# Turning B and C on VectorE instead of TensorE in a fused Mamba-2 scan and ELU feed-forward kernel

## The chip, the cores and the metric

The kernel runs on one core of a Trainium2 chip. The core has a matrix engine (TensorE, PE in the profile), three engines for elementwise work (VectorE or DVE, ScalarE or ACT, GpSimd or POOL), a queue engine (SyncE or SP) that issues most transfers here, and 16 DMA engines. The metric is the time of one execution on the device in microseconds (us); smaller is better. A figure for a kernel is the median of several executions.

## The reference: what is computed

There are two stages. The first is a state-space scan over 4 batches, 8 heads and 768 tokens, with 32 values (x) and 16 state numbers (B and C) per head and token. Written in chunks it is

```
cum   = cumsum(log a)                        # inside a chunk, per head
M     = (C @ B.T) * exp(cum_i - cum_j)       # j <= i only
y     = M @ x  +  exp(cum_i) * (C @ state)
state = exp(cum_last) * state + sum_j exp(cum_last - cum_j) * B_j x_j
```

The second stage takes the 8 heads of a token side by side as a row of 256 numbers, and computes `elu(row @ w_in) @ w_out` with `w_in` 256x2048 and `w_out` 2048x256. The weights arrive as 64-bit floats and are made into 32-bit ones on the chip; everything else is 32-bit. The output is 3072 rows of 256.

## The kernel before

**Blocks.** The work is cut into 12 blocks of 256 tokens of one batch, numbered n = 0 to 11. Blocks 2k and 2k + 1 are a pair: the same third of two batches. Inside a block the scan works on chunks of 64 tokens; u (0 or 1) says which half of 128 tokens, v which chunk in it. For each block the scan goes through these steps, each a function of its own:

- `load_bc` (L106) loads B and C into the tile `bc`, tokens on the partitions, in four transfers of 64 KB. A run in memory is 16 floats, 64 bytes. The issues are at L112.
- `scaled` (L359) multiplies B by the decay to the chunk's end, on GpSimd. It needs tokens on the partitions.
- `turn` (L368) makes the other layout, head and state number on the partitions and tokens along the row. TensorE transposes four 128x128 squares into two PSUM tiles (L374); ScalarE copies B's to `bt` (L378); VectorE makes `ctm` (L381), C's rows in two versions, each with every second head masked to zero. C itself stays in PSUM.
- `turn_exp` (L385) multiplies that C by the decay `ec` into `cts` on VectorE (L389), which frees the PSUM tile.
- `scores` (L450) multiplies `bt` and `ctm` on TensorE, `weigh` (L465) applies the decays on VectorE, `sums` and `states` (L480, L496) carry the state on, `across` and `inside` (L522, L542) make the rows of y.

**The feed-forward part** is where most of TensorE's time goes. For blocks 0 to 3 it is done directly, by `l1` (L577, first product), `elu` (L598, two steps on ScalarE and one on VectorE that writes `g`, L605) and `l2` (L700). For blocks 4 to 11 the pairs are done with a scheme of seven part products per pair instead of eight: `front`, `mid` and `back` (L660 to L692) for the first product, with sums between them on VectorE (L673, L674, L682, L689, L690), and `second` (L736) for the second product, whose results are summed up at L750. `mid` ends with the VectorE sum L682, which reads a half of a PSUM bank; `back` then accumulates into that half.

**Order.** Nothing is planned automatically: the order of the calls in the code is the order of each engine's queue. There are three parts. A start (up to L951) brings in blocks 0 to 2 and converts weights; in it a loop over s (L914) runs `l1` for blocks 0 and 1. A loop over n = 2, 3 (L1011) does `l2` of the blocks two back with `l1` of its own. The pair loop, n = 4, 6, 8, 10 (L1051), has 16 steps k. In an even step stand `front`, its sums, an `elu` and four steps of `second`; in an odd step `mid`, two steps of `second`, `back`, one step, an `elu` and the start of another. After each step `scan_ahead` (L967) puts in a piece of the scan of the coming pair: in the pair loop loads at k = 0 and 1, `turn` and `turn_exp` at k = 5 (first block of the pair) and k = 7 (second block).

The turn of blocks 6, 8 and 10 is thus at k = 5 and of blocks 7, 9 and 11 at k = 7 of the pair loop at n = 4, 6 and 8. Block 2 is turned at s = 5 of the start, block 3 at i = 1 of n = 2, blocks 4 and 5 at i = 5 and 7 of n = 2.

The first products share seven PSUM tiles (tag "a"), which `turn` also takes two of.

Of the kernel before, what the change touches and what calls it, by code (L numbers as in the profile page):

```python
# [10 lines left out]
F32 = mybir.dt.float32  # L11
U32 = mybir.dt.uint32
BF16 = mybir.dt.bfloat16
ALU = mybir.AluOpType
ACT = mybir.ActivationFunctionType

P = 128
Q = 64
BLK = 2 * P
# [9 lines left out]
def kernel(  # L29
# [27 lines left out]
    nc = tc.nc  # L57
    NB, NH, S, D = x.shape
    N = B.shape[-1]
# [4 lines left out]
    DM, DF = moe_w_in.shape  # L64
# [6 lines left out]
    raw = ctx.enter_context(tc.tile_pool(name="raw", bufs=3))  # L71
    att = ctx.enter_context(tc.tile_pool(name="att", bufs=2))
    ffn = ctx.enter_context(tc.tile_pool(name="ffn", bufs=2))
# [5 lines left out]
    def psum(shape, name):  # L79
        return p_a.tile(shape, F32, tag="a", name=name)  # L80
# [6 lines left out]
    for k in range(4):  # L87
        (nc.scalar if k % 2 else nc.sync).dma_start(
            out=la0[BH * k:BH * (k + 1)],
            in_=a.rearrange("b h (c s) -> (b h) c s", s=P)[:, 0:2, :])  # L90
# [5 lines left out]
    st = {}  # L96

    def place(n):

        return 2 * (n // (2 * NG)) + n % 2, n // 2 % NG  # L100
# [5 lines left out]
    def load_bc(n, c_queue=nc.sync):  # L106
        b, g = place(n)
        st.setdefault(n, {})["bc"] = raw.tile([P, 2, 2, NH, N], F32, tag="bc", name="bc", bufs=2)
        for u in range(2):
            sl = slice((2 * g + u) * P, (2 * g + u + 1) * P)  # L110
            for k, src in enumerate((B, C)):
                (nc.sync, c_queue)[k].dma_start(  # L112
                    out=st[n]["bc"][:, k, u], in_=src[b, :, sl, :].rearrange("h s n -> s h n"))
# [118 lines left out]
    for v in range(2):  # L232
        nc.gpsimd.affine_select(
            out=low16[Q * v:Q * v + Q], in_=low16[Q * v:Q * v + Q], pattern=[[1, Q]],
# [5 lines left out]
        out=hmask, in_=hmask, pattern=[[-N, NH]], compare_op=ALU.is_ge, fill=0.0,  # L240
        base=0, channel_multiplier=1)
    nc.gpsimd.affine_select(
        out=hmask, in_=hmask, pattern=[[N, NH]], compare_op=ALU.is_ge, fill=0.0,
# [3 lines left out]
    hmask2 = const.tile([P, 2], F32, name="hmask2")  # L247
# [4 lines left out]
        out=minus, in0=ident, scalar1=-1.0, scalar2=None, op0=ALU.mult)  # L252
# [106 lines left out]
    def scaled(n, eng):  # L359

        s = st[n]
        s["sc"] = sc = att.tile([P, 2, NH, N], F32, tag="sc", name="sc", bufs=3)
        factor = eb0[:, :, NH * n:NH * (n + 1)] if n < 2 else eb[:, :, rows_of(n)]
        eng.tensor_tensor(
            out=sc, in0=s["bc"][:, 0],
            in1=factor.unsqueeze(3).to_broadcast([P, 2, NH, N]), op=ALU.mult)

    def turn(n):  # L368

        s = st[n]  # L370
        tb, tc_ = psum([P, 2, P], "ps_tb"), psum([P, 2, P], "ps_tc")
        for k, ps in enumerate((tb, tc_)):
            for u in range(2):
                nc.tensor.transpose(  # L374
                    out=ps[:, u], in_=s["bc"][:, k, u].rearrange("p h n -> p (h n)"),
                    identity=ident)
        s["bt"] = att.tile([P, 2, P], F32, tag="bt", name="bt", bufs=3)
        nc.scalar.copy(out=s["bt"], in_=tb)  # L378
        s["ct"] = tc_
        s["ctm"] = att.tile([P, 2, 2, P], F32, tag="ctm", name="ctm")  # L380
        nc.vector.tensor_tensor(  # L381
            out=s["ctm"], in0=tc_.unsqueeze(2).to_broadcast([P, 2, 2, P]),
            in1=hmask2.unsqueeze(1).unsqueeze(3).to_broadcast([P, 2, 2, P]), op=ALU.mult)

    def turn_exp(n):  # L385

        s = st[n]
        s["cts"] = att.tile([P, 2, P], F32, tag="cts", name="cts", bufs=3)
        nc.vector.tensor_tensor(out=s["cts"], in0=s.pop("ct"), in1=s["ec"], op=ALU.mult)  # L389

# [307 lines left out]
    def l2(n, j, half=None):  # L700


        if j == 0 and half != 1:
            o_of[n] = p_o.tile([P, 2, DM], F32, tag="o", name="ps_o")
        for m in (2 * j, 2 * j + 1) if half is None else (2 * j + half,):
            for ts in range(2):
                nc.tensor.matmul(  # L707
                    out=o_of[n][:, ts], lhsT=g_of[n, j][:, m % 2, ts * P:(ts + 1) * P],
                    rhs=w_out[:, m], start=(m == 0 and ts == 0), stop=(m == MC - 1),
                    skip_group_check=True)  # L710
        if j == MC // 2 - 1 and half != 0:
            ob = ffn.tile([P, 2, DM], F32, tag="ob", name="ob")
            nc.scalar.copy(out=ob, in_=o_of.pop(n))
            r0 = row_of(n)
            nc.sync.dma_start(
                out=out[r0:r0 + BLK, :].rearrange("(t p) e -> p t e", p=P), in_=ob)
# [197 lines left out]
    for s, (n, i) in enumerate((  # L914
            (1, 0), (1, 1), (1, 2), (0, 4), (1, 3), (0, 5), (1, 4), (0, 6), (1, 5), (0, 7),
            (1, 6), (1, 7))):
        l1(n, i)
        if s < 8:
            decay_of(2, s)
        if s == 7:  # L920
            scores(2)
            weigh(2, 0)
            weigh(2, 1)
        if s % 2 == 1 and todo < 10:
            w_take(todo, nc.vector)
            w_give(todo)
            w_load(todo + 6)
            todo += 1
        if s == 4:
            scaled(2, nc.gpsimd)  # L930
        if s == 5:
            turn(2)
            first_exp(2)
            turn_exp(2)
        if s == 8:
            spread_cum(3)
            load_x(3)
            spread_exp(3)
            weigh(2, 2)
            weigh(2, 3)  # L940

            st[0] = kept
            sums(2, 0, pool=p_o, tag="o", parts=(None, last))
            states(0, last)
            st.pop(0)
            states(2)
        if s == 10:
            spread_cum(4)
            inside(across(2), 2)
        if len(lag) > 1:  # L950
            elu()  # L951
# [15 lines left out]
    def scan_ahead(n, i):  # L967


        m = n + 2 + n % 2  # L970
        if 4 < m < NP and n % 2 == 1 and i in (4, 5):
            spread_cum(m + i - 4)
        m = n + 2 - n % 2
        if 4 <= m < NP and n % 2 == 0:
            if i < 2:
                load_bc(m + i)
                spread_exp(m + i)
            if i == 2:
                if m == 4:
                    spread_cum(5)  # L980
                load_x(m)
                load_x(m + 1)
            for k in (i,) if m == 4 else (i, i + 1) if i % 2 == 0 else ():
                if k >= 2:
                    decay(m + k // 6, (k - 2) % 4)
            if i in (5, 7):
                turn(m + i // 7)
                turn_exp(m + i // 7)
        if 4 <= m < NP and n % 2 == 1:
            if i == 0:  # L990
                scaled(m, nc.gpsimd)
                scaled(m + 1, nc.gpsimd)
            for k in (i,) if m == 4 else (i, i + 1) if i % 2 == 0 else ():
                if k < 2:
                    decay(m + 1, k + 2)
            if i == 2 and m == 4:
                scores(m, m + 1)
                sums(m, m + 1)
                for q in range(4):
                    weigh(m, q)  # L1000
                    weigh(m + 1, q)
                states(m)
                states(m + 1)
# [7 lines left out]
    for n in (2, 3):  # L1011
        for i in range(8):
            l2(n - 2, i)
            if todo < len(pieces):
                w_take(todo, nc.vector)
            end_of_two(n, 2 * i)
            l1(n, i)
            if todo < len(pieces):
                w_give(todo)
                w_load(todo + 6)  # L1020
                todo += 1
            while lag:
                elu()
            if n == 2:
                if i < 2:
                    decay(3, 2 * i)
                    decay(3, 2 * i + 1)
                if i == 1:
                    scaled(3, nc.gpsimd)
                    turn(3)  # L1030
                    turn_exp(3)
                if i == 2:
                    scores(3)
                    for q in range(4):
                        weigh(3, q)
                if i == 4:
                    sums(3)
                    states(3)
                if i == 6:
                    inside(across(3), 3)  # L1040
            else:
                if i == 0:
                    s_in[:], s_out[:] = weight_sums(), weight_sums()
                elif i < 7:
                    more_sums(i - 1)
            scan_ahead(n, i)
            end_of_two(n, 2 * i + 1)
# [3 lines left out]
    for n in range(4, NP, 2):  # L1051
        m = n + 2 if n + 2 < NP else None
# [13 lines left out]
        for k in range(16):  # L1066
            i = k // 2
# [54 lines left out]
    n = NP - 2  # L1122
# [41 lines left out]
```

## Time and profile before

The median of three executions is 364.41 us (364.31 to 366.16). The profiled execution spans 362.9 us.

| Operation | Engine, line | Number | Mean of one, ns |
|---|---|---|---|
| part product 128x128, 256 columns | PE L655 | 448 | 379 to 385 |
| second product, 128 columns | PE L759 | 1120 | 275 |
| transpose 128x128 | PE L374 | 48 | 273 to 275 |
| bt, copy out of PSUM, 128x256 | ACT L378 | 12 | 358 |
| scaled B, 128x256 | POOL L364 | 12 | 655 |
| M, 128x256 | DVE L468 | 48 | 413 |
| g, 128x512 | DVE L605 | 96 | 681 |

How to read it: the page gives busy times by engine, then the chain of work that ended last, then groups of instructions. The mean of one is from its start to its end; neighbouring instructions of one engine overlap at their ends, so that the distance from start to start in the timeline is shorter than that mean, and it is that distance which adds up. A matmul of 32-bit numbers is two instructions in the profile, a transpose is one. "Idle before" is the time an engine stood still in front of an instruction, with the work that ended the stillness.

### The profile page before, as it was taken

What the parts mean: (1) busy time and instruction counts of PE and PEld (TensorE: products, weight loads), DVE (VectorE), ACT (ScalarE), POOL (GpSimd) and SP (SyncE); (2) the same over time, 40 slices, a digit from 0 to 9 for tenths busy, and PEclk for the clock granted to TensorE, in tenths of its full rate; (3) what the DMA queues carried; (4) which work ended last, traced back from release to release, by engine and by line L of the source; (5) the groups of instructions that cost most, each with busy time, mean ns of one, the idle gap of its engine ahead of it and who ended that gap; (6) DMA issues with size and microseconds to landing.
All of it is one profiled execution on the core that took longest, in us unless ns stands there. A gap on an engine that the chain in (4) does not pass through costs nothing.

```text
span 362.9 us, 10146 instructions
## 1 busy us (share of the span) xinstructions
PE 354.3 (98%) x3978; PEld 316.9 (87%) x3978; DVE 242.2 (67%) x547; ACT 200.7 (55%) x499; POOL 227.1 (63%) x366
## 2 busy tenths in 40 slices
PE   8899999999999999999999999999999999999996
PEld 5578778888888998898999998999989999999995
DVE  4989887972697668784567684666685666666212
ACT  4858969767435567635485735386735352534100
POOL 4454443663567896679457578567587555456893
PEclk9999999999999999999999999999999999999999
DMA  8877995563050560053530045540000100000001
GB/s 155 203 203 147 240 308 141 66 116 63 3 116 19 65 85 12 4 115 48 96 65 2 3 95 68 93 72 0 3 2 4 58 2 0 3 0 32 29 2 58
DMA packets 96239, 25.33 MB, mean 70 GB/s; under 512 B 77312, under 2 KB 92096, under 8 KB 96192
## 3 DMA queue, kind: packets, MB, share of 16 engines
q1 hardware_dynamic: 94016, 24.49, 33.0%
q8 instruction: 31, 0.51, 0.6%
q10 hardware_dynamic: 2176, 0.20, 0.4%
q14 instruction: 16, 0.13, 0.1%
HBM read 21.33 MB, written 3.34 MB: 68 GB/s over the span
## 4 chain that ended last, share of the span: by engine, by line
PE 81%; DVE 7%; ACT 3%; DMA 3%; SPq 2%; issue 2%; POOL 1%; ACTq 0%; DVEq 0%
PE ps_o L759 32%; PE ps_h L655 25%; PE ps_h L583 10%; PE ps_o L707 8%; SPq L112 2%; PE ps_g L459 1%; DMA w<-in_moe_w_in_dram 1%; DVE g L605 1%; PE ps_y L553 1%; ACT e L596 1%; PE ps_st L489 1%; ACT e L603 1%; DMA flat<-F 1%; DVE mag L183 1%; PE ps_y L534 1%
## 5 line engine op out<-in xcount | busy, mean ns | idle before, releaser
L596 ACT ACTIVATE e<-ps_h 128x512 f32<-128x512 f32 x96 | 56.5, 588 | 93.1 <-DVE ps_h L689 71.2
L605 DVE SCALAR_TENSOR_TENSOR g<-e,ps_h 128x512 f32<-128x512 f32 x96 | 65.3, 681 | 39.2 <-ACT e L603 35.8
L759 PEld LDWEIGHTS ps_o<-w_out,g 128*128 128x128 f32 x640 | 80.3, 192 | 3.3 <-issue 0.5
L759 PE MATMUL ps_o<-w_out,g 128*128 128x128 f32 x640 | 81.4, 275 | 0.0
L727 POOL TENSOR_TENSOR g<-g 128x256 f32<-128x256 f32 x34 | 24.8, 729 | 67.1 <-DVE g L605 67.1
L583 PE MATMUL ps_h<-yT,w_in 128*128 128x256 f32 x256 | 60.6, 383 | 2.5 <-POOL w_in L200 1.8
L603 ACT ACTIVATE e<-e 128x512 f32<-128x512 f32 x96 | 60.9, 634 | 2.2
L583 PEld LDWEIGHTS ps_h<-yT,w_in 128*128 128x128 f32 x256 | 47.8, 190 | 10.6 <-POOL w_in L200 2.8
L759 PE MATMUL ps_o<-w_sum,g 128*128 128x128 f32 x320 | 43.0, 275 | 0.0
L759 PEld LDWEIGHTS ps_o<-w_sum,g 128*128 128x128 f32 x320 | 41.1, 192 | 1.4
L439 ACT ACTIVATE L<-L,ncum 128x64 f32<-128x64 f32 x160 | 41.0, 338 | 0.0
L655 PE MATMUL ps_h<-y_sum,w_in 128*128 128x256 f32 x128 | 38.6, 383 | 0.7 <-DVE ps_h L682 0.7
L655 PE MATMUL ps_h<-y_sum,w_sum 128*128 128x256 f32 x128 | 38.5, 382 | 0.5 <-DVE g L605 0.5
L655 PE MATMUL ps_h<-yT,w_in 128*128 128x256 f32 x128 | 38.8, 385 | 0.0
L444 POOL TENSOR_SCALAR_AFFINE_SELECT L<-L 64x512 f32<-64x512 f32 x40 | 27.3, 682 | 13.1 <-ACT L L439 11.8
L707 PE MATMUL ps_o<-w_out,g 128*128 128x256 f32 x128 | 30.8, 383 | 0.0
L655 PEld LDWEIGHTS ps_h<-y_sum,w_sum 128*128 128x128 f32 x128 | 23.9, 190 | 5.3 <-DVE g L605 1.3
L723 POOL TENSOR_TENSOR g<-t,g 128x256 f32<-128x256 f32 x40 | 27.9, 729 | 0.8 <-PE ps_o L759 0.8
L723 POOL TENSOR_TENSOR t<-g 128x256 f32<-128x256 f32 x40 | 28.1, 736 | 0.2
L723 POOL TENSOR_TENSOR g<-g,t 128x256 f32<-128x256 f32 x40 | 27.9, 730 | 0.2
L707 PEld LDWEIGHTS ps_o<-w_out,g 128*128 128x128 f32 x128 | 23.7, 190 | 3.4 <-POOL L L444 0.2
L689 DVE TENSOR_TENSOR ps_h<-ps_h,u_sum 128x256 f32<-128x256 f32 x32 | 13.7, 429 | 18.3 <-PE ps_h L655 18.3
(109 smaller groups left out, 538.3 us busy)
## 6 DMA issues: line engine op xcount, KB each, us to landing
L<-flat SPq DMA_DIRECT2D x20, 256.0 KB, 5.3
w<-in_moe_w_in_dram SPq DMA_DIRECT2D x8, 512.0 KB, 5.2
w<-in_moe_w_out_dram SPq DMA_DIRECT2D x8, 512.0 KB, 6.1
xr<-in_x_dram SPq DMA_DIRECT2D x24, 128.0 KB, 3.4
out_dram<-c_sum SPq DMA_DIRECT2D x10, 256.0 KB, 2.1
bc<-in_B_dram SPq DMA_DIRECT2D x24, 64.0 KB, 4.4
bc<-in_C_dram SPq DMA_DIRECT2D x22, 64.0 KB, 3.4
ec<-flat_exp SPq DMA_DIRECT2D x72, 16.0 KB, 1.7
```

Source lines behind the costliest of these rows:

```text
L439: nc.scalar.activation(L[:, h, u], L[:, h, u], ACT.Exp, bias=ncum[:, u, row:row + 1])
L444: nc.gpsimd.affine_select(out=part, in_=part, pattern=[[0, 4], [0, 2], [1, Q]], compare_op=ALU.is_ge, fill=0.0, base=0, channel_multiplier=-1)
L583: nc.tensor.matmul(out=ps[:, j], lhsT=w_in[:, k, m * P:(m + 1) * P], rhs=yT[n // 2][:, k, n % 2].rearrange("p u i -> p (u i)"), start=(k = ...
L596: nc.scalar.activation(begun[0], lag[0][2], ACT.Relu, scale=-1.0)
L603: nc.scalar.activation(e, e, ACT.Exp, scale=-1.0)
L605: nc.vector.scalar_tensor_tensor(out=g_of[n, i], in0=e, scalar=1.0, in1=ps, op0=ALU.subtract, op1=ALU.max)
L655: nc.tensor.matmul(out=out, lhsT=lhsT, rhs=rhs, start=first, stop=True, skip_group_check=True)
L689: nc.vector.tensor_tensor(out=c1[:, 1], in0=c1[:, 1], in1=u[:, 0], op=ALU.add)
L707: nc.tensor.matmul(out=o_of[n][:, ts], lhsT=g_of[n, j][:, m % 2, ts * P:(ts + 1) * P], rhs=w_out[:, m], start=(m == 0 and ts == 0), stop=( ...
L723: nc.gpsimd.tensor_tensor(out=out, in0=in0, in1=in1, op=ALU.subtract)
L727: eng.tensor_tensor(out=b12, in0=b12, in1=g_of[n, i][:, 0], op=ALU.subtract)
L759: nc.tensor.matmul(out=ps[:, ts], lhsT=b[:, ts * P:(ts + 1) * P], rhs=a[:, i], start=(i == chunk[0] and ts == 0), stop=(i == chunk[-1]), s ...
```

## The change

From block 2 on, B and C are brought in a second layout which VectorE can turn by itself. VectorE's transpose works on squares of 32x32 numbers, so the new transfer places the data such that these squares are enough: a partition is one of four head pairs and one of 32 runs of 8 tokens, and a row holds the 8 tokens times 16 state numbers of both heads of the pair. A run in memory is then 512 bytes. Two instructions, one for C and one for B, turn a block, and write with a step of 8 numbers, so that the tokens come out in order.

- `load_bc`: from block 2 on, B is loaded as before into a tile of its own, `b` (two transfers, for `scaled`), and B and C as squares into `bc` (four transfers): six issues and 384 KB in place of four and 256 KB.
- `turn_squares` takes the place of `turn`: two VectorE transposes into one tile, `bct` (two buffers, in place of three of `bt`), then `ctm` on VectorE from that tile in SBUF.
- `turn_exp` reads C from the same tile; for block 2 it is on GpSimd.
- Block 2 is turned at s = 4 instead of 5, block 3 at s = 10 of the start instead of i = 1 of n = 2. The others keep their places.
- The tile `ob` (first two blocks' output) has one buffer instead of two.

The aim is to free TensorE of these transposes, ScalarE of the copy and PSUM of two tiles per block.

```diff
@@ load_bc
+        if n > 1:
+            st[n]["b"] = raw.tile([P, 2, NH, N], F32, tag="b", name="b_tok", bufs=2)
+            for u in range(2):
+                sl = slice((2 * g + u) * P, (2 * g + u + 1) * P)
+                nc.sync.dma_start(
+                    out=st[n]["b"][:, u], in_=B[b, :, sl, :].rearrange("h s n -> s h n"))
+            squares = st[n]["bc"].rearrange("p k u h n -> p k (u h n)").rearrange(
+                "p k (m r) -> p k m r", m=2)
+            for k, src in enumerate((B, C)):
+                for m in range(2):
+                    nc.sync.dma_start(
+                        out=squares[:, k, m],
+                        in_=src[b, m:NH:2, g * BLK:(g + 1) * BLK, :].rearrange(
+                            "q (c t) n -> q c (t n)", t=8))
+            return
@@ scaled
-            out=sc, in0=s["bc"][:, 0],
+            out=sc, in0=s["b"] if n > 1 else s["bc"][:, 0],
@@ turn (still used for blocks 0 and 1)
-        s["bt"] = att.tile([P, 2, P], F32, tag="bt", name="bt", bufs=3)
+        s["bt"] = att.tile([P, 2, 2, P], F32, tag="bct", name="bct", bufs=2)[:, 0]
@@ turn_exp takes the engine as an argument (VectorE if none is given)
+    def turn_squares(n):
+        s = st[n]
+        t = att.tile([P, 2, 2, P], F32, tag="bct", name="bct", bufs=2)
+        squares = s["bc"].rearrange("p k u h n -> p k (u h n)").rearrange(
+            "p k (m t n) -> p k t m n", m=2, n=N)
+        for k in (1, 0):
+            nc.vector.transpose(
+                out=t[:, k].rearrange("p u i -> p (u i)").rearrange("p (c t) -> p t c", t=8),
+                in_=squares[:, k])
+        s["bt"], s["ct"] = t[:, 0], t[:, 1]
+        s["ctm"] = att.tile([P, 2, 2, P], F32, tag="ctm", name="ctm")
+        nc.vector.tensor_tensor(
+            out=s["ctm"], in0=s["ct"].unsqueeze(2).to_broadcast([P, 2, 2, P]),
+            in1=hmask2.unsqueeze(1).unsqueeze(3).to_broadcast([P, 2, 2, P]), op=ALU.mult)
@@ start, loop over s
         if s == 4:
             scaled(2, nc.gpsimd)
+            turn_squares(2)
+        if s == 10:
+            turn_squares(3)
         if s == 5:
-            turn(2)
             first_exp(2)
-            turn_exp(2)
+            turn_exp(2, nc.gpsimd)
@@ scan_ahead
             if i in (5, 7):
-                turn(m + i // 7)
+                turn_squares(m + i // 7)
                 turn_exp(m + i // 7)
@@ n = 2, i = 1
                     scaled(3, nc.gpsimd)
-                    turn(3)
                     turn_exp(3)
```

More of the change, by code (lines that the diff above doesn't have):

```diff
@@ L383, in turn, with turn_exp @@
             in1=hmask2.unsqueeze(1).unsqueeze(3).to_broadcast([P, 2, 2, P]), op=ALU.mult)
-    def turn_exp(n):
+    def turn_exp(n, eng=nc.vector):
         s = st[n]
         s["cts"] = att.tile([P, 2, P], F32, tag="cts", name="cts", bufs=3)
-        nc.vector.tensor_tensor(out=s["cts"], in0=s.pop("ct"), in1=s["ec"], op=ALU.mult)
+        eng.tensor_tensor(out=s["cts"], in0=s.pop("ct"), in1=s["ec"], op=ALU.mult)
+    def turn_squares(n):
[12 more added lines that the diff above has]
+            in1=hmask2.unsqueeze(1).unsqueeze(3).to_broadcast([P, 2, 2, P]), op=ALU.mult)
     def first_low(n, last=None):
@@ L711, in l2 @@
         if j == MC // 2 - 1 and half != 0:
-            ob = ffn.tile([P, 2, DM], F32, tag="ob", name="ob")
+            ob = ffn.tile([P, 2, DM], F32, tag="ob", name="ob", bufs=1)
             nc.scalar.copy(out=ob, in_=o_of.pop(n))
```

## The prediction

> **What bounds the kernel now.** I read the page's busy line first, then its chain that ended last.
>
> ```profile
> PE 354.3 (98%) x3978; PEld 316.9 (87%) x3978; DVE 242.2 (67%) x547; ACT 200.7 (55%) x499; POOL 227.1 (63%) x366
> ...
> PE 81%; DVE 7%; ACT 3%; DMA 3%; SPq 2%; issue 2%; POOL 1%; ACTq 0%; DVEq 0%
> ```
>
> TensorE sets the time; from about 53 us on its products follow one another almost without a gap. A change gains by taking work from TensorE, and loses by making TensorE wait. Next, the groups that the edit touches, shapes kept apart:
>
> ```profile
> L381 DVE TENSOR_TENSOR ctm<-ps_tc,hmask 128x512 f32<-128x512 f32 x12 | 8.2, 682 | 0.2 <-PE ps_tc L374 0.2
> ...
> L389 DVE TENSOR_TENSOR cts<-ps_tc,ec 128x256 f32<-128x256 f32 x12 | 5.0, 414 | 0.3 <-ACT ec L357 0.3
> L374 PE MATMUL ps_tb<-ident,bc 128*128 128x128 f32 x24 | 4.6, 275 | 0.0
> ...
> L374 PE MATMUL ps_tc<-ident,bc 128*128 128x128 f32 x24 | 4.6, 273 | 0.0
> ```
>
> A duration of 275 ns is not what a transpose costs in a pipelined stream. The chain around block ten shows the cost:
>
> ```profile
> 247.93 0.45 PE ps_o L759 x4
> 248.37 0.22 PE ps_tb L374 x2
> 248.59 0.22 PE ps_tc L374 x2
> 248.81 1.30 PE ps_h L655 x6
> ```
>
> Four transposes take 0.44 us of TensorE. Then I asked what stands next to them on VectorE, in the timeline of block six's turn (blocks count from 0), the first in the pair loop (n = 4):
>
> ```profile
> 138.47 0.69 DVE L605 SCALAR_TENSOR_TENSOR g<-e,ps_h 128x512 f32<-128x512 f32 x1
> ...
> 139.07 0.68 DVE L381 TENSOR_TENSOR ctm<-ps_tc,hmask 128x512 f32<-128x512 f32 x1
> ...
> 139.67 0.41 DVE L389 TENSOR_TENSOR cts<-ps_tc,ec 128x256 f32<-128x256 f32 x1
> ...
> 140.79 0.68 DVE L605 SCALAR_TENSOR_TENSOR g<-e,ps_h 128x512 f32<-128x512 f32 x1
> 141.39 0.42 DVE L750 TENSOR_TENSOR c_sum<-ps_o,p_sum 128x256 f32<-128x256 f32 x1
> ...
> 141.72 0.42 DVE L682 TENSOR_TENSOR ps_h<-ps_h,u_sum 128x256 f32<-128x256 f32 x1
> 142.20 0.30 PEld L655 LDWEIGHTS ps_h<-y_sum,w_in 128*128 128x128 f32 x2 [0.86 <-DVE ps_h L682]
> ```
>
> VectorE runs without a pause from g at 138.47 to L682 at 141.72, and TensorE stands idle for its result. L682 reads the half of a PSUM bank into which the next product (`back`) accumulates, so that product cannot start sooner. This is the one place in the pair loop where VectorE leads TensorE, and the turn is what fills it. The turns at k = 5 for blocks eight and ten show the same unbroken VectorE run, but L682 ends just in time (197.61 us, weights loaded at 197.71). The second turn of each pair, at k = 7, has some slack:
>
> ```profile
> 202.54 0.68 DVE L605 SCALAR_TENSOR_TENSOR g<-e,ps_h 128x512 f32<-128x512 f32 x1
> ...
> 203.72 0.43 DVE L682 TENSOR_TENSOR ps_h<-ps_h,u_sum 128x256 f32<-128x256 f32 x1 [0.50 <-PE ps_h L655]
> ...
> 204.30 0.30 PEld L655 LDWEIGHTS ps_h<-y_sum,w_in 128*128 128x128 f32 x2
> ```
>
> [...] the same 128x128 sum takes 0.28 us free and 0.71 us when it meets a running GpSimd instruction, ending 0.23 us after that one.
>
> ```profile
> 137.38 0.28 DVE L631 TENSOR_TENSOR w_sum<-w_out 128x128 f32<-128x128 f32 x1
> 137.44 2.94 POOL L723 TENSOR_TENSOR t<-g 128x256 f32<-128x256 f32 x4
> 137.69 0.71 DVE L631 TENSOR_TENSOR w_out<-w_out 128x128 f32<-128x128 f32 x1
> ```
>
> **Removed.** Ten turns of 0.44 us of TensorE: 4.4 us if nothing else moves. Also ten ScalarE copies of bt (358 ns, L378), which lie beside other work, and two PSUM tiles per turn.
>
> **Added on VectorE.** Two transposes of 128x256 per block. Their price T, start to start: from below 0.34 us, the spacing of 256-element operations here (139.67 to 140.00 is 0.33). From above 0.60 us, the spacing of 512-element ones (138.47 to 139.07)[...]. The transposes write with a step of 8 floats, 32 bytes, [...] I take 0.50 us, 1.0 us for two. ctm and cts keep their spacing (0.60 and 0.33) but read both inputs from SBUF[...].
>
> **Moved to where VectorE is full: the six pair-loop turns.** The transposes stand behind g and ahead of ctm, cts, the u sums, the next g and L682.
> - k = 5, block six: ctm would start at 139.07 + 1.0 = 140.07; the last of GpSimd's four subtractions ends at 137.44 + 2.94 = 140.38, so it waits 0.31. TensorE waits already, so 1.3 us comes on top, and the 0.44 us saved ahead of the wait only lengthens it: +1.3.
> - k = 5, blocks eight and ten: ctm at 194.54 + 1.0, GpSimd done at 192.70 + 2.79 = 195.49, so no lock wait. +1.0 less 0.1 of slack: +0.9 each.
> - k = 7, three blocks: VectorE is free at 202.54 + 0.60 = 203.14; 1.0 later L682 starts at 204.14, its result is there 0.48 later (as 141.72 to 142.20), at 204.62 instead of 204.30: +0.3 each.
> Sum: 1.3 + 1.8 + 0.9 = **+4.0 us**. The whole saving of TensorE in these six turns (2.6 us) is inside these figures.
>
> **The first four turns** (blocks two to five, before 117 us) gain, because VectorE's stretches there have room: idle 1.59 us before g at 53.92 hides block three's new place, and 1.57 and 2.28 us after the turns of blocks four and five hide theirs. Block two's 1.6 us on VectorE replace 0.94 us further on, in a stretch with 1.0 us idle; its cts goes to GpSimd (0.7 us, needed 10 us later). Four times 0.44 is 1.76. I add 0.1 each for blocks three and four, where TensorE waits briefly for bt's copy or for the PSUM tile that cts frees, and 0.1 for block two: **-2.1 us**.
>
> **Costed at nothing.** DMA: per block, 4096 packets of 64 B become 2048 of 64 B and 512 of 512 B. That is lighter, and helps the queue around 25 to 35 us, where one B load holds SyncE for 4.3 us; yet TensorE is busy there from 27.55 to 42.4, so hardly anything of it arrives. Loads land some 10 us ahead of the turns. The two buffers of the shared bt/ct tile: two blocks back, all readers are done. The single ob buffer: its two uses lie a whole block apart.
>
> Net: 364.4 + 4.0 - 2.1 = about **366.4 us**.
>
> **Rivals.** *Same* (0.34): [...] T = 0.34. With lock waits, k = 5 costs 1.3 + 0.86 + 0.87, k = 7 nothing, net +0.9: 365.4. Without any lock wait 0.68 + 0.58 + 0.58, net -0.3: 364.1. [...] Against: the 32-byte steps.
> *Faster* (0.14): VectorE's delay does not reach TensorE, and all ten turns gain: 364.4 - 4.4 - 0.3 = 359.7; if only half of it arrives, 362. For it: VectorE is busy only 67%. Against: that is an average, and the wait at 142.20 names VectorE at just this place.
> *Much slower* (0.14): T = 0.6 to 0.8 and lock waits. At 0.6: 1.3 + 2.2 + 1.6 = 5.1, 367.4; at 0.8: 7.4, 369.7.
>
> **How the numbers follow.** My forecast has 0.38: the VectorE queue bounds all six pair-loop turns at T of about 0.5. About an eighth of that chance lies within half a per cent (under 366.2). Faster 0.14; same 0.34 + 0.05 = 0.39; slower 0.33 + 0.14 = 0.47. The range leaves out the faster case and the upper part of the worst: 363.0 to 368.8.
>
> **What would show it.** Transposes at 0.34, 0.5 or 0.6 us from start to start settle T. PE waits on L682 of about 1.5 us (three of them or more) ahead of `back` after k = 5, and smaller ones after k = 7, show the moved bound; no such waits, and a TensorE stretch of about 4 us less, show the rival. Before 117 us the same products should come about 2 us sooner. ctm at more than 0.7 us beside GpSimd's L723 shows the lock. I am wrong if transposes are below 0.3 us, if something else hides the queue, or if the DMA change speeds the start by more than 1 us.

## The result and the profile after

The changed kernel takes **378.57 us** (median of four executions, 377.36 to 379.96), the kernel before 364.85 beside it: ratio 1.0376, 95% interval 1.0341 to 1.0410. It is 13.7 us slower; 366.4 was predicted, with a range up to 368.8.

From the page of the kernel after: the busy line, one of the two DMA queues that it calls instruction (packets, MB, share), and the chain that ended last.

```profile
PE 355.2 (94%) x3938; PEld 316.2 (84%) x3938; DVE 254.6 (67%) x566; ACT 198.0 (52%) x489; POOL 228.9 (61%) x367
...
q8 instruction: 31, 0.51, 0.6%
...
PE 63%; DVE 9%; POOL 9%; SPq 6%; DMA 5%; issue 5%; ACT 3%; DVEq 0%; ACTq 0%; POOLq 0%
```

The span grew from 362.9 to 377.4 us, yet TensorE is busy about as long as before (354.3 then). So the time went into pauses of TensorE and, as the windows below show, into two stretches at half clock. Its share of the chain fell from 81% to 63%. SyncE's queue, transfers and "issue" (waits for nothing the profile names) rose from 7% to 16% together, GpSimd from 1% to 9%, VectorE from 7% to 9%. So VectorE's queue is unlikely to be all of the loss.

The groups of the turn, shapes kept apart (L416 the transposes, L421 the masks, L406 the decayed C):

```profile
L416 DVE STREAM_TRANSPOSE bct<-bc 128x256 f32<-128x256 f32 x20 | 11.1, 634 | 0.0
L421 DVE TENSOR_TENSOR ctm<-bct,hmask 128x512 f32<-128x512 f32 x10 | 7.7, 774 | 0.0
L406 DVE TENSOR_TENSOR cts<-bct,ec 128x256 f32<-128x256 f32 x9 | 5.3, 592 | 0.0
```

ctm and cts were 682 and 414 ns when C lay in PSUM; now they are 774 and 592 in the mean.

To find where the time went I took the 96 instructions that write `g`, which both kernels have in the same order, and read how much later each starts than before. The delay, in one profiled execution of each, grows in four places and is flat between them:

| Stretch (time before) | Delay at its end, us | Growth | What stands there in the trace of after |
|---|---|---|---|
| start to 81 us | 0.96 | +0.96 | waits on VectorE, and its longer times beside GpSimd, against the turns spared |
| 81 to 90 us | 5.10 | +4.14 | TensorE waits 3.1 us for a copy behind a late transfer, then a slow clock |
| turns at n = 4, 6, 8 | | +1.84, +1.58, +1.56 | waits on L716 (L682 before) and on the sums |
| near 231 and 280 us | 14.22 | +0.51, +3.63 | TensorE stops inside `inside`, with no cause named, then a slow clock |

*The turns in the pair loop.* The timeline of block six's turn at n = 4 (L639 is g, L716 the sum before `back`):

```profile
143.56 0.69 DVE L639 SCALAR_TENSOR_TENSOR g<-e,ps_h 128x512 f32<-128x512 f32 x1
144.17 1.12 DVE L416 STREAM_TRANSPOSE bct<-bc 128x256 f32<-128x256 f32 x2
...
145.13 0.89 DVE L421 TENSOR_TENSOR ctm<-bct,hmask 128x512 f32<-128x512 f32 x1
...
147.99 0.42 DVE L716 TENSOR_TENSOR ps_h<-ps_h,u_sum 128x256 f32<-128x256 f32 x1
...
148.47 0.70 PE L689 MATMUL ps_h<-y_sum,w_in 128*128 128x256 f32 x2 [2.11 <-DVE ps_h L716]
```

Two transposes take 145.13 - 144.17 = 0.96 us, 0.48 each from start to start. ctm stretches to 0.89 beside GpSimd's four subtractions, where in before, with C in PSUM, it took 0.68 beside the same four. Such longer times beside GpSimd are the lock waits of the recorded texts (in the prediction 0.71 us for a sum of 0.28); what makes them longer no run here tests. TensorE's product waits 2.11 us, where in before it waited 0.67 (its weights, shown above, 0.86).

*The pause near 87 us.* In the kernel before, SyncE issued the decay rows L of block five at this time:

```profile
76.64 1.27 SPq L335 DMA_DIRECT2D L<-flat  x2
```

In the kernel after the issue is 4 us later:

```profile
80.71 1.30 SPq L352 DMA_DIRECT2D L<-flat  x2
```

and ScalarE and TensorE of after do this (L473 is the decay, L747 the copy into `ob`, L741 the second product):

```profile
87.04 1.06 ACT L473 ACTIVATE L<-L,ncum 128x64 f32<-128x64 f32 x4 [3.61 <-DMA L<-flat]
88.01 0.56 ACT L747 COPY ob<-ps_o 128x512 f32<-128x512 f32 x1
...
88.63 2.77 PE L741 MATMUL ps_o<-w_out,g 128*128 128x256 f32 x8 [3.13 <-ACT ob L747]
```

The copy needs nothing from L; it only stands behind the waiting decay in ScalarE's queue, and TensorE needs the PSUM tile that it empties. The mean granted clock is 0.71 from 88 to 92 us and 0.86 in the next four: it is 0.50 from 89.70 to 93.11 us, and 1.00 on either side. Over that stretch the delay of TensorE's products grows by about 1.7 us, which is some two fifths of the 4.14.

*The stop near 285 us.* TensorE in `inside` (L587), and then the windows (the column after POOL is the granted clock):

```profile
283.71 1.04 PE L587 MATMUL ps_y<-M,xr 64*32 64x64 f32 x80
286.48 0.71 PE L587 MATMUL ps_y<-M,xr 64*32 64x64 f32 x48 [1.73 <-issue]
```

```profile
286.00:288.00 2.00, 1.52 (x54) 1.43 (x54) 0.00 (x0) 0.80 (x3) 2.00 (x3) 0.92 0.03 8
288.00:290.00 2.00, 2.00 (x8) 1.73 (x7) 0.00 (x0) 0.30 (x1) 1.55 (x3) 0.50 0.00 0
```

TensorE stops for 1.73 us in the middle of a run of 128 small products, with no wait that the profile names, and behind it works at half speed (0.50), from 287.67 to 291.09 us, which again adds about 1.7 us. A packet of q8 starts at 283.8 us, as the burst begins. There are 31 such packets of 16 KB, and TensorE has 7,876 instructions: about 254 to a packet, if q8 brings TensorE's alone (the last four packets, 316.9 to 367.1 us, start 254 of TensorE's instructions apart). The kernel before runs the same burst in 1.51 us without a stop.

### The profile page after: what moved, and what is told of

It is laid out like the page before. It is cut to its first block, busy times and chain, and to the rows that moved or that the text cites. A ratio compares the mean times of both kernels' runs of the same rounds, so it can differ in the third digit from the quotient of the medians.

```text
span 377.4 us, 10105 instructions
## 1 busy us (share of the span) xinstructions
PE 355.2 (94%) x3938; PEld 316.2 (84%) x3938; DVE 254.6 (67%) x566; ACT 198.0 (52%) x489; POOL 228.9 (61%) x367
## 3 DMA queue, kind: packets, MB, share of 16 engines
q1 hardware_dynamic: 78496, 25.80, 30.2%
## 4 chain that ended last, share of the span: by engine, by line
PE 63%; DVE 9%; POOL 9%; SPq 6%; DMA 5%; issue 5%; ACT 3%; DVEq 0%; ACTq 0%; POOLq 0%
PE ps_o L793 27%; PE ps_h L689 21%; PE ps_o L741 6%; PE ps_h L617 5%; POOL g L757 3%; SPq L137 3%; SPq L121 2%; PE ps_y L587 2%; DMA L<-flat 1%; DMA w<-in_moe_w_in_dram 1%; DMA bc<-in_C_dram 1%; DVE cts L406 1%; SPq L362 1%; POOL sc L381 1%; DVE mag L200 1%
## 5 line engine op out<-in xcount | busy, mean ns | idle before, releaser
L639 DVE SCALAR_TENSOR_TENSOR g<-e,ps_h 128x512 f32<-128x512 f32 x96 | 65.3, 682 | 37.4 <-ACT e L637 33.9
L617 PE MATMUL ps_h<-yT,w_in 128*128 128x256 f32 x256 | 61.2, 387 | 2.3 <-ACT yT L604 1.6
L617 PEld LDWEIGHTS ps_h<-yT,w_in 128*128 128x128 f32 x256 | 48.7, 193 | 10.4 <-POOL w_in L217 3.1
L473 ACT ACTIVATE L<-L,ncum 128x64 f32<-128x64 f32 x160 | 41.1, 337 | 5.9 <-DMA L<-flat 5.9
L793 PE MATMUL ps_o<-w_sum,g 128*128 128x128 f32 x320 | 43.9, 279 | 0.0
L793 PEld LDWEIGHTS ps_o<-w_sum,g 128*128 128x128 f32 x320 | 42.0, 195 | 1.6
L689 PE MATMUL ps_h<-yT,w_in 128*128 128x256 f32 x128 | 39.3, 389 | 0.1
L741 PE MATMUL ps_o<-w_out,g 128*128 128x256 f32 x128 | 31.8, 393 | 3.8 <-ACT ob L747 3.1
L741 PEld LDWEIGHTS ps_o<-w_out,g 128*128 128x128 f32 x128 | 24.0, 192 | 8.5 <-ACT ob L747 3.5
L689 PEld LDWEIGHTS ps_h<-y_sum,w_in 128*128 128x128 f32 x128 | 21.8, 190 | 8.4 <-DVE ps_h L716 6.7
```

The source lines that it names most:

```text
L473: nc.scalar.activation(L[:, h, u], L[:, h, u], ACT.Exp, bias=ncum[:, u, row:row + 1])
L617: nc.tensor.matmul(out=ps[:, j], lhsT=w_in[:, k, m * P:(m + 1) * P], rhs=yT[n // 2][:, k, n % 2].rearrange("p u i -> p (u i)"), start=(k = ...
L639: nc.vector.scalar_tensor_tensor(out=g_of[n, i], in0=e, scalar=1.0, in1=ps, op0=ALU.subtract, op1=ALU.max)
L689: nc.tensor.matmul(out=out, lhsT=lhsT, rhs=rhs, start=first, stop=True, skip_group_check=True)
L741: nc.tensor.matmul(out=o_of[n][:, ts], lhsT=g_of[n, j][:, m % 2, ts * P:(ts + 1) * P], rhs=w_out[:, m], start=(m == 0 and ts == 0), stop=( ...
L793: nc.tensor.matmul(out=ps[:, ts], lhsT=b[:, ts * P:(ts + 1) * P], rhs=a[:, i], start=(i == chunk[0] and ts == 0), stop=(i == chunk[-1]), s ...
```

## The experiments

My theory after the result: four separate causes, (i) the order on SyncE's queue, (ii) VectorE's queue in the pair loop, (iii) the place of TensorE's instructions in the stream that q8's packets bring, (iv) no gain in the first four turns. The rival: VectorE's delays alone, of which the other pauses are echoes. The ratios are to the kernel before, beside which each ran.

| Kernel | us | Ratio (95%) |
|---|---|---|
| e1_pad: after, 24 tiny products more | 373.01 | 1.0212 (1.0196 to 1.0227) |
| e2_order: after, L ahead of ec | 372.55 | 1.0205 (1.0176 to 1.0233) |
| e3_flat: after, transposes write contiguously | 376.53 | none (371.4 to 378.0) |
| e4_early: after, transposes ahead of the ELU | 373.46 | 1.0195 (1.0141 to 1.0249) |
| e5_slots: e2, turn spread over idle places | 367.99 | 1.0058 (1.0018 to 1.0098) |
| e6_slots_pad: e5, 24 tiny products more | 366.72 | 1.0042 (1.0023 to 1.0060) |
| e7_loads: before, two loads more per block | 372.21 | 1.0192 (1.0153 to 1.0231) |
| e8_first4: e2, only blocks 2 to 5 on VectorE | 366.01 | 1.0028 (1.0012 to 1.0044) |
| e9_parity: after, the stream filled up | 374.87 | 1.0257 (1.0215 to 1.0298) |
| e10_slots_parity: e5, the stream filled up | 365.75 | 1.0026 (1.0015 to 1.0037) |
| e11_best: e10, block two as before | 365.38 | 1.0020 (1.0009 to 1.0031) |
| e12_before_pad: before, 44 tiny products more | 371.52 | 1.0194 (1.0153 to 1.0234) |

### SyncE's queue: e2 and e7

e2 changes the order of two groups of issues:

```diff
             if i < 2:
                 load_bc(m + i)
-                spread_exp(m + i)
+                if (m, i) != (4, 1):
+                    spread_exp(m + i)
             if i == 2:
                 if m == 4:
                     spread_cum(5)
+                    spread_exp(5)
```

> The changed kernel with block five's eight decay loads (ec) issued after its large decay load (L) instead of ahead of it. Theory A (the pause of 3.5 us at 85 us comes from SyncE's queue, some 4 us late by then, so that L of block five lands late and holds up ScalarE's queue, behind which the output copy stands): L lands some 3 us sooner, the pause and the slow clock behind it go, and the time falls by 4 to 5 us, to about 374. Theory B (the copy waits because the ob tile has one buffer): no change, 378 to 379.

372.55 us, 6.0 less than after. The pause is gone; `g` behind it comes 0.71 us earlier than in before, where after was 5.10 late. At this place alone, from 81 to 90 us, after loses 4.14 us and e2 gains 0.94. The decay now starts in time, so the wait was for the transfer and not for VectorE.

e7 asks the reverse, in the kernel before: nothing but two more loads per block and the single `ob` buffer.

```diff
+        if n > 1:
+            more = raw.tile([P, 2, P], F32, tag="b", name="b_more", bufs=2)
+            for m in range(2):
+                nc.sync.dma_start(
+                    out=more[:, m],
+                    in_=B[b, m:NH:2, g * BLK:(g + 1) * BLK, :].rearrange(
+                        "q (c t) n -> q c (t n)", t=8))
...
-            ob = ffn.tile([P, 2, DM], F32, tag="ob", name="ob")
+            ob = ffn.tile([P, 2, DM], F32, tag="ob", name="ob", bufs=1)
```

> The kernel before, all its turns on TensorE, with two more transfers of B per block from block two on (128 KB each block into a tile that nobody reads) and one ob buffer: six issues and 384 KB per block as in after, none of its VectorE work. Theory A (the longer row of issues on SyncE makes the late transfer of L by itself): the transfer for block five leaves 3 to 4 us later than before, ScalarE waits for it near 85 us with the copy into ob behind it, TensorE stops about 3 us; 368 to 370. Theory B (what I costed at nothing is nothing; the pause comes from VectorE's delays): no such pause, 364.5 to 366.

372.21 us, more than either theory gave. In its trace (L446 the decay, L714 the second product):

```profile
90.93 1.06 ACT L446 ACTIVATE L<-L,ncum 128x64 f32<-128x64 f32 x4 [6.02 <-DMA L<-flat]
...
92.52 3.78 PE L714 MATMUL ps_o<-w_out,g 128*128 128x256 f32 x8 [5.11 <-ACT ob L720]
```

The same pause, longer (5.11 us), with the issue of L at 85.59 in place of 76.64, and not one VectorE instruction of the change in the kernel. In the profiled execution `g` is 1.93 us late ahead of this place and 9.15 behind it, and the delay then stays flat to the end. Theory A holds: without any of the change's VectorE work the queue makes the pause. Two points limit this. e7 has the single `ob` buffer too; e2 keeps that buffer and has no pause, so the buffer alone does not make it, but e7 does not try the loads without it. And e7's loads are not quite after's: four with runs of 64 bytes and two with 512, where after has two and four. On the queue, two x loads hold SyncE for 9.62 us (9.02 in after, 7.67 in before), and what is added ahead pushes all behind it; why a hold lasts so long no run here shows.

### VectorE in the pair loop: e3, e4, e5

e3 lets the transposes write without the step; the tokens then stand in another order, which changes the numbers that come out but no amount of work.

```diff
-                out=t[:, k].rearrange("p u i -> p (u i)").rearrange("p (c t) -> p t c", t=8),
+                out=t[:, k].rearrange("p u i -> p (u i)").rearrange("p (t c) -> p t c", t=8),
```

> The changed kernel with the transposes writing their 256 numbers side by side instead of with a step of 8: the tokens of blocks 2 to 11 come out in a wrong order, so the output is not the reference's; all else is the same. Theory A (the 32-byte step is what makes a transpose 634 ns long, 0.48 us from start to start): 450 ns long, 0.34 from start to start, and the six pair-loop turns lose 0.28 us less each, 1.5 to 2 us in all: about 376.8. Theory B (a 32-bit transpose costs that in any case): 634 ns as before, time unchanged.

Its executions lie too far apart for a ratio; the trace answers. The same group of e3, to set beside that of after:

```profile
L416 DVE STREAM_TRANSPOSE bct<-bc 128x256 f32<-128x256 f32 x20 | 7.6, 420 | 0.0
```

420 ns for 634: the step of 32 bytes costs 214 ns on each transpose. The delay that the six turns add falls from 5.0 to 3.8 us, the stops without a named cause left out in both. So price and queue are linked as I had argued, but the price of the step is only about a quarter of this loss.

e4 takes the twelve transposes of the pair loop out of the queue ahead of L716 (one each ahead of the ELU at k = 3, 5, 7, 9), and leaves ctm and cts where they are.

```diff
             if i in (5, 7):
-                turn_squares(m + i // 7)
+                (turn_squares if m == 4 else mask_c)(m + i // 7)
                 turn_exp(m + i // 7)
...
+                if m and k in (3, 5, 7, 9):
+                    turn_part(m + (k - 3) // 4, 1 - (k - 3) // 2 % 2)
```

> The changed kernel with the twelve pair-loop transposes one at a time at k = 3, 5, 7 and 9, ahead of the ELU step, where VectorE stands idle for 0.5 to 1.0 us waiting for ScalarE; the masks and the decay product stay at k = 5 and 7. Theory A (the transposes in front of L682 are what makes TensorE wait in the pair loop): TensorE's waits on L682 fall from 2.1 and 1.2 us to below 0.6, and the time falls by 3 to 5 us, to about 374.5. Theory B (the loss in the pair loop comes from ctm and cts reading SBUF beside GpSimd): at most 1 us comes back.

The pair loop loses 2.3 us against before (4.23 to 6.52 of delay), where after lost 5.5; stops without a named cause are 0.6 and 0.5 us of these. (e4 takes 5.1 us less than after. The pair loop is 3.2 of it; the pause near 87 us and the stop near 282 us, with no half clock behind them in e4, cost 1.7 and 1.9 us less.) The waits at k = 7 go; those at k = 5 stay, 0.8 to 2.0 us, and the trace of e4 shows why (L764 is GpSimd's subtractions, L428 ctm):

```profile
198.34 3.25 POOL L764 TENSOR_TENSOR t<-g 128x256 f32<-128x256 f32 x4
...
200.18 0.82 DVE L428 TENSOR_TENSOR ctm<-bct,hmask 128x512 f32<-128x512 f32 x1
...
200.93 0.95 DVE L406 TENSOR_TENSOR cts<-bct,ec 128x256 f32<-128x256 f32 x1
```

Earlier by 1 us, the two now fall into GpSimd's run of four (198.34 to 201.59) and take 0.82 and 0.95 us beside it, where after has 0.66 and 0.39 at this turn (202.45 and 203.05, GpSimd idle). The mean of cts rises from 592 to 779 ns. Both theories hold in part.

e5 therefore puts every piece where the trace of after has VectorE idle and, for ctm and cts, GpSimd out of its subtractions. It has e2's order.

```diff
+    slot_a = {
+        3: lambda m: turn_part(m, 1), 5: lambda m: turn_part(m + 1, 1), 7: lambda m: mask_c(m)}
+    slot_b = {
+        3: lambda m: turn_part(m, 0), 5: lambda m: turn_part(m + 1, 0),
+        7: lambda m: mask_c(m + 1)}
...
                 l2s(2)
+                if m and k in slot_a:
+                    slot_a[k](m)
                 back(n, i)
...
                 l2s(1)
+                if m and k in slot_b:
+                    slot_b[k](m)
                 next_elu()
```

> The order of e2, and in the pair loop the four transposes and the masks stand singly in places where VectorE was idle in the trace of after (C of the first block between mid and back at k = 3, B ahead of the ELU there, the second block's at k = 5, the masks at k = 7, the decayed C at k = 7 where GpSimd has paused). Theory A (transposes in the queue ahead of L682, and lock waits of ctm and cts beside GpSimd, are all that the six turns lose): no wait of TensorE on L682's result over 0.5 us at k = 5 and 7, pair loop 5 to 7.5 us shorter than in after; with the 5.1 us of e2's order 378.6 - 5.1 - 6 = 367.5, range 366 to 369, the stops without a wait (L587, 2 to 3 us) still in it. Theory B (VectorE as a whole is the bound of the pair loop, wherever its transposes stand): the waits only move, and it comes out within 1.5 us of e2, 371 to 373.

367.99 us, as theory A gave. All waits of TensorE on that sum, in e5 (L723 there):

```profile
PE ps_h L696 <- DVE ps_h L723: 0.4, 1, 0.4
```

One wait of 0.4 us where after had six, 5.5 in all. Against before, the delay goes from -0.12 at the start of the pair loop to -1.34 at the end of its turns: the six turns now gain 1.2 us, of the 2.6 that TensorE is spared. The same VectorE work made this part 5.4 us longer in e2 (-0.71 to 4.74), 0.5 of it at stops without a named cause: where it stands decides, not how much it is.

### The first four turns: e8

e8 has e2's order of issues too; the rest of its edit is

```diff
-        if n > 1:
+        if 1 < n < 6:
             st[n]["b"] = raw.tile([P, 2, NH, N], F32, tag="b", name="b_tok", bufs=2)
...
             if i in (5, 7):
-                turn_squares(m + i // 7)
+                (turn_squares if m == 4 else turn)(m + i // 7)
```

> The order of e2; blocks two to five are turned by VectorE as in after, blocks six to eleven by TensorE as before. Theory A (my step on the first four turns): 2.1 us less than before, about 363, g of the pair loop 2 us sooner than before. Theory B (from the trace of after: what TensorE is spared there is given back in waits on VectorE and its locks): within 1 us of before, 364.5 to 366, and in the pair loop no wait on L682 that before does not have. If the stops without a wait appear here too, they add 2 to 3 us to either.

366.01 us: no gain. `g` is 0.68 us late at 47 us and 0.26 early behind block five's turn, where I had said 2.1; e2 and e5, with the same code up to there, have 0.71 and 0.12 early. A later stop of 1.0 us without a wait adds 0.6. Where the spared time goes, in the trace of e8 (L493 is `scores` of block two):

```profile
38.16 1.12 DVE L416 STREAM_TRANSPOSE bct<-bc 128x256 f32<-128x256 f32 x2
...
39.13 1.09 DVE L421 TENSOR_TENSOR ctm<-bct,hmask 128x512 f32<-128x512 f32 x1
...
43.20 0.68 PE L493 MATMUL ps_g<-ctm,bct 32*64 32x128 f32 x26 [0.82 <-DVE g L639]
```

ctm takes 1.09 us here (0.66 when it is free), the weight conversions and g behind it are late, and TensorE stops 0.82 us for the g that frees its PSUM tile. Block two's turn costs more than the 0.44 it saves.

### The instruction stream: e1, e6, e9, e10, e12

e1 puts 24 products of one number each behind the warming product of the start: 96 instructions of TensorE in the profile.

```diff
     idle_product(3)
+    for _ in range(24):
+        nc.tensor.matmul(
+            out=ps_idle[0:1, 0, 0:1], lhsT=idle[:, 0:1], rhs=idle[:, 0:1], start=True, stop=True)
```

> The changed kernel with 24 tiny matmuls (1 by 1, 96 TensorE instructions) put into TensorE's pause near 11 us, so that TensorE's later instructions stand at other places of their instruction stream, about where the kernel before had them. Theory A (the stops of 0.95 us at 231 us and 1.73 us at 285 us, for which the profile names no releaser, and the slow clock behind the second, come from TensorE running out of fetched instructions in a dense burst of short products): both stops move or go, and the time falls by 3 to 4 us, to about 374.5; the same bursts take 1.4 us again. Theory B (the stops are waits for data of the scan, which came late in the changed kernel): they stay in place, and the time stays at 378 to 379.

373.01 us, 5.6 less than after although work was added. The stops near 231 and 285 are gone (the growth there is 0.00 and 0.01 us in place of 0.51 and 3.63); one of 1.52 us appears at 14 us, right behind the added products, with half clock from 13.93 to 20.75 us. The start is so 3.9 us later, and the pause near 87 us is gone with it, since the products are then later and the transfer is not (L of block five is issued at 80.28 us): so the total of this run can't separate the two.

e6 is e5 with the same padding.

> e5 and 24 more tiny products at the start (96 instructions of TensorE), as in e1. Theory A (the stops of TensorE in L587 that no wait explains hang on where its instruction stream is fetched): the stops move or go, 2 to 4 us less than e5, 363 to 366, no wait marked issue of over 1 us near 231 and 285 us. Theory B (they come from the data or the queue of work around L587): the stops stay at the same instructions and the time is e5's or up to 2 us more.

366.72 us: the stop of 1.9 us in e5 goes, but one of 2.6 us comes at 14 us, right behind the added products. The total hardly differs from e5's, and the intervals overlap; but the stops move with the count. That is against theory B and shows that padding at the start is no cure.

e9 therefore fills up exactly: two tiny products (eight instructions) where each of the ten turns stood (eight instructions).

```diff
+    def fill(k):
+        t = psum([P, 2, P], "ps_fill")
+        for _ in range(k):
+            nc.tensor.matmul(
+                out=t[0:1, 0, 0:1], lhsT=ident[:, 0:1], rhs=ident[:, 0:1], start=True, stop=True)
...
             if i in (5, 7):
+                fill(2)
                 turn_squares(m + i // 7)
```

> The kernel after with two tiny 1x1 products on TensorE where each of its ten removed turns stood: eight instructions of TensorE for eight, so that its instruction stream is as long as before's at every point, at 0.1 us a turn in place of 0.44. Nothing else changed. Theory A (the stops without a wait hang on where the instruction stream is fetched, and before had them nowhere because of its length): the stops near 231 and 285 us go, and with them the slow clock behind the second: 378.6 - 0.5 - 3.6 = 374.5. Theory B (the stops come from after's other delays): they stay, 378 to 380.

374.87 us, 374.5 expected. The burst that stopped in after, in e9 (L593 is `inside`):

```profile
283.85 1.51 PE L593 MATMUL ps_y<-M,xr 64*32 64x64 f32 x128
```

All 128 in 1.51 us without a break, and no growth of the delay at either place. The pause near 87 us is still there (3.1 us), and so are the turns' waits, as they should be.

> The same filling in e5. Theory A: e5's stop of 1.9 us near 273 us and the slow clock behind it go (3.8 us in e5's trace), 368.0 - 3.8 = 364.2, a little under the kernel before. Theory B: the stop stays or moves, 366 to 368.

e10 takes 365.75 us, and its ratio is 1.0026 where e5 had 1.0058; the intervals overlap, so it is the trace that shows the effect: the delay no longer grows near 280 us (3.76 us in e5). It misses 364.2: in its profiled execution the start is 1.2 us later, with half clock from 13.62 to 17.03 us. With the three remedies (order, idle places, filled stream) 0.3% is left of the 3.8% that the change cost.

e12 provokes the stop in the kernel before. Its TensorE has 176 instructions more than before's, where after's has 80 fewer. The two are 256 apart, about one packet by the 254 that the trace of after gives, so by this estimate they stand at about the same place of a packet:

```diff
+            if n == 3 and i % 2 == 0:
+                fill(11)
             l2(n - 2, i)
```

> The kernel before with 44 tiny products (176 instructions of TensorE, four groups of eleven in the loop n = 3): after's stream is 80 instructions shorter than before's[...]. Cost of the products themselves 2 to 2.5 us. Theory A (place in the instruction stream alone): a stop of 1 to 2 us without a wait in L553 near 280 to 285 us and perhaps a smaller one near 230, with a slow clock behind: 365 + 2.3 + 2 to 4 = 369.5 to 371.5. Theory B: no such stop, 367 to 368.

371.52 us, at the upper end of theory A; but the 44 products cost 3.3 us and not 2 to 2.5, so the trace has to decide. Its TensorE in the same burst (L559 is `inside`):

```profile
276.72 0.97 PE L559 MATMUL ps_y<-M,xr 64*32 64x64 f32 x73
279.40 0.88 PE L559 MATMUL ps_y<-M,xr 64*32 64x64 f32 x55 [1.71 <-issue]
```

A stop of 1.71 us behind the 73rd of 128 products, in the kernel after behind the 80th, and 3.55 us of growth against 3.63, in a kernel that has nothing of the change. The place in the instruction stream is enough to make the stop.

### A version of all this: e11

e11 is e10 with block two loaded and turned as before (`if n > 2`, `turn(2)` at s = 5).

> e10, and block two loaded and turned as in the kernel before, on TensorE, so that VectorE's 1.6 us of its turn at s = 4 and its decayed C on GpSimd go. Theory A (block two's turn costs more than it saves: in the trace of e8 the products from 47 us on come 0.68 us later than in before): 0.7 us less than e10, 363.0 to 363.8, the pair loop's end 1.5 to 2 us before the kernel before's. Theory B (the early delays come from block three's turn or from the loads): as e10 or slower.

365.38 us, 0.2% above the kernel before. Block two's loss does go (`g` is 0.69 us early at 47 us instead of 0.80 late in e5), but it is lost again at once:

```profile
52.77 1.13 PE L630 MATMUL ps_h<-yT,w_in 128*128 128x256 f32 x4 [1.02 <-issue]
```

The kernel before waits 0.18 us with no cause named at this instruction and is 0.7 us later there. Up to this point the two streams of TensorE have equal lengths (1,444 instructions), so length alone isn't all. In e11 the products ahead are 0.65 us earlier, while the packet of q8 starts at 50.28 us, in before at 50.02: how fast the instructions are used up seems to count as well, which no run tests by itself. I have no version that beats the kernel before.

## Why the prediction was wrong, point by point

- *TensorE bounds the kernel; ten turns of 0.44 us are spared*: right. Its busy time stays within 1 us (354.3 and 355.2), and each spared turn shows as a step of -0.43 or -0.44 where nothing stands against it (e8, at 58 and 90 us).
- *T = 0.50 us with a penalty for the 32-byte step*: right, 0.48. (The 0.50 was an estimate between the two spacings, 0.34 and 0.60; no trace of before has a VectorE transpose.) Without the step 420 ns instead of 634 (e3). The rival at 0.34 is out.
- *The six turns, +4.0*: the mechanism was right, and by turn so were the sizes. At k = 5 the delay grew 1.17, 0.89 and 0.90 us (1.3, 0.9, 0.9 said), at k = 7 about 0.25 each (0.3 said). Missed: at the head of the next stretch 0.43 us a pair, since GpSimd follows the late g and its `sc` is late for TensorE's `sums` (0.32 us of wait at 216.96). Sum 5.0. (One reading of a lock wait was a little off: the GpSimd instruction at 137.44 ran 0.81 us, so the sum beside it ended 0.15 us after it and not 0.23.)
- *The first four turns, -2.1*: wrong; with the loads in order they gain 0.1 to 0.7 us (e5, e8, e2), and in after nothing is left of it. I looked for room in VectorE's idle time behind the turns, and priced no lock wait there, though I had read one in the trace of before: ctm took 1.09 us for 0.66, a conversion behind it 0.90 for 0.45. The 0.2 us that I allowed for block two's cts on GpSimd was not the term that mattered.
- *Costed at nothing: DMA*: wrong, the largest miss, 5.1 us (4.14 lost for 0.94 gained). I counted packets and bytes in the loads that grew, found them lighter (q1's packets did fall from 94,016 and 33.0% of 16 engines' span to 78,496 and 30.2%), and looked at the landing of these loads. I did not follow the queue behind them to its latest member: L of block five, issued at 76.64 us and used by ScalarE at 83.00, 6.4 us later, with a copy behind it that TensorE needs. From its issue to its use in after, with ScalarE waiting, it is 6.3 us (80.71 to 87.04): there was no slack to lose, and both numbers for before stood in its trace. I named a wait's followers for every VectorE wait but not for this one. e7 shows that it needs none of the VectorE work. About 1.7 us of the 4.14 is the half clock behind the pause.
- *Not in the prediction at all: the instruction stream*: 4.1 us of after's delay, about 1.7 of it the half clock behind the second stop. None of my cases had it, and the kernel before shows no such stop: there the packets of q8 start 1.15 to 1.52 us behind the first product of a burst of 128, which is then nearly over. The range could only have held it if I had counted the 80 instructions removed as a change of their own.
- *The range to 368.8*: it took in the unknown price of a transpose, the smallest of the doubts. Of the 12.2 us between 366.4 and 378.6, SyncE's queue is 5.1, the instruction stream 4.1, the first four turns 2.1 and the pair loop 1.0.

## What to carry to other kernels

When a change adds transfers to a queue, find the transfer behind them that is used soonest after its issue, and what stands behind its user (here L of block five, 6.3 us from issue to use, and a pause of 3.1 us); bytes and packets don't show that. Work moved to an engine that is busy 67% of the time is free or costly by its place: the same six turns cost about 5 us in one order and gained 1.2 in another, and ctm and cts took 0.82 and 0.95 us beside GpSimd's subtractions (e4) for 0.66 and 0.39 with GpSimd idle (after). If a change alters how many instructions TensorE has, fill the stream up to the old length once, cheaply: what then disappears (in e9 the 4.1 us of delay at the two stops) was the layout and not the idea.

## What the runs showed of the hardware that I had not expected

- *Stops for instructions.* A burst of 128 products takes 1.51 us in e9 without a break; in it TensorE stopped for 1.71 us in e12 and for 1.73 in after. The packets of q8 in all 14 traces tell more. Each of the 22 pauses of TensorE over 0.3 us for which the profile names no releaser ends 1.2 to 1.7 us after the end of a packet of q8 (after's of 0.95 and 1.73 us end 1.42 and 1.46 us behind one). Of the 56 bursts of 128 products, 18 took 1.97 us or more, and in each of them a packet starts between 1.34 us ahead of the first product and 0.31 us behind it; the other 38 took 1.51 to 1.54 us, and in none of them does a packet start there. That TensorE waits for the fetched instructions is still inferred from these times and from the runs that moved the stop; no line names it.
- *A slow clock behind short stops, but not behind each.* In every trace the granted clock changes only at points 3.41 us or a multiple of it apart, and each slow stretch inside a kernel lasts 3.41 or 6.83 us (in after 89.70 to 93.11 and 287.67 to 291.09). In the 3.41 us ahead of these two TensorE was idle for 2.34 and 1.73 us, so not for all of such a window. Nor does the length of the stop decide. e4 has the pause near 87 us too (in the window, the column after POOL is the granted clock):

```profile
89.44 1.99 PE L748 MATMUL ps_o<-w_out,g 128*128 128x256 f32 x8 [3.09 <-ACT ob L754]
```

```profile
88.00:92.00 4.00, 2.56 (x12) 2.27 (x13) 1.42 (x3) 3.47 (x11) 0.43 (x1) 1.00 0.58 125
```

It is as long as after's, 3.09 us, but a border of these windows, at 88.30 us (counted back from e4's clock change at 371.60), parts it into 1.95 and 1.15 us; the clock stays at 1.00, and the place costs 2.4 us where after lost 4.1. (In e2 the stop of 1.45 us near 280 us had none and cost 1.70 us where after lost 3.63.) Idle time in a window doesn't decide it alone either, since 1.71 us in e12 had a slow clock behind it and 1.95 in e4 had none; beside the first stood thin work of 64x64 products, and whether that is the reason no run here tests.

- *Transposes with a step*: 634 ns (after) against 420 ns without it (e3) for 128x256 numbers of 32 bits, at equal work.
